# Fused attention and gated two-layer product on one core: held output sums, early units, split differences, and Tile's scheduler for all engines but TensorE

## The chip, the cores and the metric

The kernel runs on one core of a Trainium2 chip. The core has a TensorE (PE, with its weight loads listed apart as PEld), a VectorE (DVE), a ScalarE (ACT), a GpSimd (POOL), a SyncE (SP) that here only issues transfers, and 16 DMA engines. The metric is device time in microseconds (us). Before the change the median of three runs was 1395.18 us (1393.9 to 1398.31).

## The reference

The inputs are q, k and v of 8 batches x 8 heads x 576 positions x 64 numbers, and the weights w_in (512 x 2048) and w_out (2048 x 512), all float32.

```python
scores = scale * np.matmul(q, k.transpose(0, 1, 3, 2))      # scale = 1/8
mask = block_i >= block_j                                   # blocks of 64 positions
scores = np.where(mask, scores, -1000000000.0)
scores = scores - np.max(scores, axis=-1, keepdims=True)
attn = np.exp(scores)
attn = attn / (np.sum(attn, axis=-1, keepdims=True) + 1e-09)
x = np.matmul(attn, v)          # heads side by side: 4608 tokens x 512
h = x @ w_in
sp = np.maximum(h, 0.0) + np.log1p(np.exp(-np.abs(h)))
out = (h * erf(sp)) @ w_out
```

All products keep float32 accuracy. The kernel reaches it by splitting each number into a high part, which the cheap format holds exactly, and a low part, the difference; a product is then three products (high x high, high x low, low x high) added up in PSUM.

## The kernel before, in words

**Attention.** The 64 heads are 64 slots, n = 0 to 63. For head n, `load_qk` brings k and q into one of four buffers (st and qk): SP issues the loads and two copies (L450, L452, L453), POOL one load (L451), and POOL subtracts to get the low parts (kl at L456, ql at L457). `maxes` multiplies scores (s, L468), takes row maxima on DVE (L472, joined at L498), transposes them on PE (L502), and ACT copies them out of PSUM (mt, L504) and issues a transfer (L505) that puts them beside q as one more row of the contraction. The mask is also rows of that kind. `probs` then multiplies the transposed scores with the maxima already taken off (t, L521 and L522), ACT takes the exponential (p, L528) into one of two float32 buffers p32_0 (128 x 832) and p32_1 (128 x 768), and `split` makes the high half ph on ACT (L536) and the low half pl on DVE (L537), both in 16 bits. There is one copy of each p32 buffer. For a pair of heads `pv` multiplies by v (u, L567), and sums the rows (us, L593). Every four heads `normalise` transposes the sums and takes their reciprocal (rt L611, ri L614), spreads it (rw, ACT copies L621; transposes rb L629), multiplies (xs, DVE L632), splits the result (xs again: cast on ACT L634, difference on POOL L635) and sends it to DRAM (x_d, L636).

**The two-layer product.** w_in and w_out are cut into 16 weights of 128 hidden columns. `load_weight` splits each: SP loads it (raw, L285), DVE takes its bits apart (bits and sq, L287 to L297, ten operations of 128 x 512 for one weight), ACT squares and casts (L291, whi at L299) and POOL finishes the low part (wlo, L300 and L301). The work is done in two phases.

- Phase one holds 6 weights and runs over 18 tiles of 256 tokens. A tile has 3 units of 2 weights. A unit goes up (m_h, L342: 24 multiplications into one PSUM bank), through the gate, and down (o, L363: 12 multiplications into the tile's two output banks). The result of a tile is a partial sum; `store` copies it (ob, L670) to DRAM (part_d).
- Phase two holds the other 10 weights and runs over 9 tiles of 512 tokens, a unit being one weight. It adds the partial sums and writes the output.

The gate approximates h x erf(softplus(h)): ACT takes a tanh (L314) and four squares (L320), DVE joins (L324) and multiplies by h (L328), ACT casts to the high part gh (L329), POOL subtracts for the low part gl (L330).

**What sets the order.** Every instruction is a task with an engine, an estimated duration, its dependencies and a priority (`add`). `Plan.order` plays all tasks through a model of the engines: a free engine takes the ready task of lowest priority number, a result reaches another engine 200 ns after (`HOP`), and PE or a freed PSUM bank 500 ns later still (`SPARE`). The program is then written out in the model's order of start times, under a `manual_schedule`, so each engine issues in just that order. The eight PSUM banks and the numbered buffers are handed out in that model too. The last loop but one sets the priorities: slot n's steps lie between n and n + 1, the six weights of phase one are split in slots 1, 2, 3, 4, 7 and 8 (`W1`), and phase-one units are spread evenly over the slots by `spread`; those that are left when the heads end follow behind them. The five last of them (`TAIL`) use buffers that open only after attention.

## Time and profile before

| what | before |
|---|---|
| runs, median (lowest to highest) | 1395.18 us (1393.9 to 1398.31) |
| the profiled execution | 1394.03 us |
| its span, first to last instruction | 1392.3 us |
| mean granted TensorE clock | 0.922 |
| PE busy | 1254.5 us, 90% |
| PEld busy | 1038.4 us, 75% |
| DVE busy | 804.2 us, 58% |
| ACT busy | 973.5 us, 70% |
| POOL busy | 591.1 us, 42% |

The profile is of one execution; its times are counted from the first instruction. A group of instructions is named by its line in the kernel before, its engine, what it writes and what it reads, with buffer numbers left out. The granted clock says at what share of its full speed TensorE was let run in a stretch of time, and a duration of a multiplication is read together with it. A busy share of the whole span mixes stages in which different engines are the bound; the prediction therefore cuts the span into stages.

### The profile page before, as it was taken

The numbers are of one execution on the slowest core, as the hardware profiler recorded it, in microseconds if no ns is written. First come the engines' busy times: TensorE is split into PE (matmuls) and PEld (weight loads), VectorE is DVE, ScalarE is ACT, GpSimd is POOL, SyncE is SP. The second block draws the span as 40 slices with busy tenths as digits, with TensorE's granted clock in tenths as the row PEclk, the third lists the DMA queues.
The fourth block names the chain that finished last, engine by engine and source line by source line (L and its number), as shares of the span: only waits on it lengthen the run. The fifth ranks groups of instructions, "written<-read, shape, count | busy, mean of one in ns | idle before, by whom it ended". The sixth has DMA issues, their size and how long they took to land.

```text
span 1392.3 us, 22070 instructions
## 1 busy us (share of the span) xinstructions
PE 1254.5 (90%) x8168; PEld 1038.4 (75%) x8168; DVE 804.2 (58%) x1237; ACT 973.5 (70%) x1781; POOL 591.1 (42%) x456
## 2 busy tenths in 40 slices
PE   7456688889998999999999998779999999999997
PEld 3345576677777778788989987568888888888885
DVE  4988867888777788886532218953333233333232
ACT  1445557788776787789877768557677676776764
POOL 5666545576564566654432225632222222222221
PEclk9756778899999999999999999889999999999999
DMA  9556376787767677753473223203203113113010
GB/s 238 150 139 161 94 201 170 185 209 204 190 181 176 169 199 207 179 158 124 154 255 105 91 76 137 76 2 120 99 23 122 61 61 121 61 61 121 1 61 31
DMA packets 89372, 179.97 MB, mean 129 GB/s; under 512 B 8540, under 2 KB 27292, under 8 KB 89264
## 3 DMA queue, kind: packets, MB, share of 16 engines
q1 hardware_dynamic: 79280, 159.41, 38.5%
q0 software_dynamic: 9344, 18.97, 6.5%
q8 instruction: 65, 1.06, 0.3%
q10 hardware_dynamic: 640, 0.17, 0.1%
q14 instruction: 43, 0.35, 0.1%
HBM read 112.29 MB, written 37.75 MB: 108 GB/s over the span
## 4 chain that ended last, share of the span: by engine, by line
PE 53%; DVE 5%; ACT 2%; issue 1%; DMA 1%; DVEq 0%; ACTq 0%
PE o L363 25%; PE m_h L342 24%; DVE bits L287 1%; DVE bits L289 1%; PE u L567 1%; DVE m_r L324 1%; DMA qk<-mt 1%; PE t L521 1%; ACT m_r L320 1%; PE t L522 1%; PE s L468 1%; DVE sq L292 0%; DVE pl L537 0%; DVE bits L295 0%; PE rt L611 0%
## 5 line engine op out<-in xcount | busy, mean ns | idle before, releaser
L320 ACT ACTIVATE m_r<-m_r,c 128x512 f32<-128x512 f32 x576 | 406.3, 720 | 88.1 <-DVE m_r L324 61.6
L330 POOL TENSOR_TENSOR m_gl<-m_r,m_gh 128x512 fp32r<-128x512 f32 x144 | 189.0, 1314 | 511.8 <-ACT m_gh L329 298.4
L324 DVE SCALAR_TENSOR_TENSOR m_r<-m_r,m_r 128x512 f32<-128x512 f32 x144 | 125.6, 873 | 289.7 <-ACT m_r L320 268.7
L342 PE MATMUL m_h<-xh,whi 128*128 128x256 f32 (+1 forms) x648 | 208.9, 322 | 0.1
L342 PE MATMUL m_h<-xl,whi 128*128 128x256 f32 (+1 forms) x648 | 207.4, 320 | 0.0
L342 PE MATMUL m_h<-xh,wlo 128*128 128x256 f32 (+1 forms) x648 | 207.3, 320 | 0.0
L472 DVE TENSOR_REDUCE mx<-s 64x1 f32<-64x288 f32 (+4 forms) x384 | 163.9, 464 | 61.2 <-PE s L468 60.5
L528 ACT ACTIVATE p<-t 128x288 f32<-128x288 f32 (+4 forms) x384 | 135.3, 386 | 74.1 <-PE t L522 32.6
L363 PE MATMUL o<-whi,m_gh 128*128 128x512 f32 x432 | 173.7, 402 | 14.6 <-ACT m_gh L329 14.3
L521 PE MATMUL t<-qk 69*128 69x288 f32 (+4 forms) x384 | 136.3, 359 | 45.0 <-DMA qk<-mt 15.5
L328 DVE SCALAR_TENSOR_TENSOR m_r<-m_r,m_h 128x512 f32<-128x512 f32 x144 | 98.7, 685 | 134.5 <-ACT m_r L320 134.5
L363 PE MATMUL o<-wlo,m_gh 128*128 128x512 f32 x432 | 172.6, 400 | 0.0
L537 DVE TENSOR_TENSOR pl<-p,ph 128x832 f16<-128x832 f32 (+1 forms) x128 | 151.6, 1186 | 28.9 <-ACT ph L536 28.6
L468 PE MATMUL s<-qk 68*128 68x256 f32 (+3 forms) x384 | 119.4, 372 | 42.6 <-DVE mx L472 24.9
L314 ACT ACTIVATE m_r<-m_h,c 128x512 f32<-128x512 f32 x144 | 98.5, 684 | 78.1 <-PE m_h L342 77.2
L456 POOL TENSOR_TENSOR qk<-st,qk 64x576 fp32r<-64x576 f32 x64 | 106.6, 1669 | 69.8 <-DMA qk<-qk 40.0
L457 POOL TENSOR_TENSOR qk<-st,qk 64x576 fp32r<-64x576 f32 x64 | 108.1, 1688 | 60.9 <-DMA qk<-qk 57.7
L342 PEld LDWEIGHTS m_h<-xh,whi 128*128 128x128 f32 x648 | 124.5, 192 | 10.9 <-DVE mx L472 0.4
L342 PEld LDWEIGHTS m_h<-xl,whi 128*128 128x128 f32 x648 | 124.5, 192 | 10.0
L342 PEld LDWEIGHTS m_h<-xh,wlo 128*128 128x128 f32 x648 | 124.3, 192 | 8.5
L522 PE MATMUL t<-qk 128*128 128x288 f32 (+4 forms) x384 | 126.2, 333 | 0.0
L363 PE MATMUL o<-whi,m_gl 128*128 128x512 f32 x432 | 126.1, 394 | 0.0
(83 smaller groups left out, 2357.9 us busy)
## 6 DMA issues: line engine op xcount, KB each, us to landing
st<-qk SPq DMA_DIRECT2D x64, 288.0 KB
qk<-qk POOLq DMA_DIRECT2D x64, 288.0 KB, 4.8
qk<-qk SPq DMA_DIRECT2D x64, 288.0 KB
x_d<-xs SPq DMA_DIRECT2D x32, 576.0 KB
raw<-w SPq DMA_DIRECT2D x32, 512.0 KB
v<-v SPq DMA_DIRECT2D x16, 640.0 KB
qk<-qk SPq DMA_DIRECT2D x64, 144.0 KB
xh<-x_d SPq DMA_DIRECT2D x18, 512.0 KB
```

Source lines behind the costliest of these rows:

```text
L320: add("ACT", 722, lambda r=r, a=a, pp=pp: nc.scalar.activation(r[0](), a[0](), AF.Square, bias=const(pp[1]), scale=pp[0]), r=[a[1]], w=[r[1]])
L324: add("DVE", 890, lambda r=r, a=a, c=c, pp=pp, ops=ops: nc.vector.scalar_tensor_tensor(out=r[0](), in0=a[0](), scalar=pp[0], in1=c[0](), o ...
L330: add("POOL", 1450, lambda: nc.gpsimd.tensor_tensor(out=bgl(), in0=g[0](), in1=f32(bgh()), op=ALU.subtract), r=[g[1], bgh], w=[bgl])
L342: nc.tensor.matmul(hk()[:, k, :], lhsT=a(0)[:, cc * P : (cc + 1) * P], rhs=x()[:, cc, :], start=cc == 0 and i == 0, stop=cc == NCC - 1 and ...
L363: nc.tensor.matmul(o[c](), lhsT=a()[:, sl], rhs=b_(1), start=first and k == 0 and not lo and b_ is whi, stop=last and k == nu - 1 and lo)
L457: add("POOL", 1780, lambda: nc.gpsimd.tensor_tensor(out=t[D:, 1, :], in0=st()[D:, :], in1=f32(t[D:, 1, :]), op=ALU.subtract), r=[st], w=Q( ...
L468: add("PE", mmns(w_), lambda: nc.tensor.matmul(s()[:r, c0 : c0 + w_], lhsT=qh[:K, i * P : i * P + r], rhs=kh[:K, k0 : k0 + w_], start=True ...
L472: add("DVE", 145 + 1.07 * w_, lambda: nc.vector.tensor_reduce(out=mx[:r, col : col + 1], in_=s()[:r, c0 : c0 + w_], axis=AX.X, op=ALU.max, ...
L521: nc.tensor.matmul(s()[:kk, :w_], lhsT=kh[:K, ks], rhs=qh[:K, q0 : q0 + w_], start=True, stop=False)
L522: nc.tensor.matmul(s()[:kk, :w_], lhsT=klh[:, ks], rhs=qhl[:, q0 : q0 + w_], start=False, stop=True)
L528: add("ACT", 160 + 0.84 * (w_ - skip), lambda: nc.scalar.activation(p32s[pt][:kk, c : c + w_ - skip], s()[:kk, skip:w_], AF.Exp, scale=SCALE),
L537: add("DVE", 1250, lambda: nc.vector.tensor_tensor(out=pl(), in0=p, in1=ph(), op=ALU.subtract), r=keys + [ph], w=[pl])
```

## The change

The change has six parts.

- **Who orders.** `manual_schedule` now names PE alone. PE still issues in the order of the plan; for ACT, DVE, POOL and SP the scheduler of Tile, the layer in which the kernel is written, chooses the order.
- **Priorities in the plan.** `SPARE` is 300 in place of 500. ACT and DVE tasks that read PSUM go ahead by 0.7 (`DRAIN`), gates by 8 in place of 3 (`GATE`), PV products by 1.2 in place of 0.7.
- **Early units.** Phase-one units are no longer spread over the slots. They get priorities behind all attention work (`FILL` + their number), so the plan fills PE's gaps with them as early as their inputs are there; their gates get 10 + 1.1 for each unit. The weights of phase one are split in slots 2, 4, 6 and 8, and the last two when their first unit is planned.
- **Held sums.** For the first 14 tiles (`HT`) the down products of all three units are put off until the last unit's gate is planned, and are then written sorted by output bank.
- **Buffers.** Each p32 buffer exists twice (`NP`), gh and gl four times (`NG`, three before), r0 and r1 twice (`NR`, three before), xs once (`NX`, two before), ob once (two before). The gate no longer uses gl's buffer for an intermediate value.
- **Split differences.** pl of p32_0 stays on DVE, pl of p32_1 (128 x 768) goes to POOL. The rw copies and the xs cast go from ACT to DVE. The 16-bit unit matrix id16 is no longer made; its only use, the warming products at the start, read the other one's bytes.

```diff
-    SPARE = 500.0
+    SPARE = 300.0
+    DRAIN = -0.7
...
+        if eng in ("ACT", "DVE") and any((k[0] if isinstance(k, tuple) else k).tag[1] == "PSUM" for k in r if isinstance(k[0] if isinstance(k, tuple) else k, Buf)):
+            t.prio += self.DRAIN
...
-    GATE = -3.0
+    GATE = -8.0
+    NG, NR = 4, 2
+    HT = 14
+    NP = (2, 2)
+    NX = 1
...
-        bgh, bgl = (buf(gpool, [P, n], F32R, t, f"{name}_{t}") for t in ("gh", "gl"))
-        br = [buf("m", [P, n], F32, t, f"{name}_{t}") for t in ("r0", "r1")]
-        regs = [(br[0], br[0])]
-        free = [((lambda: f32(bgl())), bgl), (br[1], br[1])]
+        bgh, bgl = (buf(gpool, [P, n], F32R, t, f"{name}_{t}", NG if gpool == "m" else None) for t in ("gh", "gl"))
+        br = [buf("m", [P, n], F32, t, f"{name}_{t}", NR) for t in ("r0", "r1")]
+        regs, free = [(br[0], br[0])], [(br[1], br[1])]
...
-        plan.prio = at + GATE
+        plan.prio = at + GATE if when is None else when
...
-        for a in sorted(((k, c, lo) for k in range(nu) for c in range(tw // P) for lo in (False, True)),
-                        key=lambda a: (a[2], a[0], a[1]) if spread else (a[1], a[2], a[0])):
+        steps = [(a[1], lambda a=a: down(*a)) for a in sorted(((k, c, lo) for k in range(nu) for c in range(tw // P) for lo in (False, True)),
+                                                           key=lambda a: (a[2], a[0], a[1]) if spread else (a[1], a[2], a[0]))]
+        if held is not None:
+            held.extend(steps)
+            if not last:
+                return
+            steps = sorted(held, key=lambda s: s[0])
+            held.clear()
+        for c, f in steps:
             plan.prio += rate
-            down(*a)
+            f()
...
-    p32s = [spool.tile([P, n], F32, name=f"p32_{i}") for i, n in enumerate(PN)]
+    p32s = [[spool.tile([P, n], F32, name=f"p32_{i}_{j}") for j in range(NP[i])] for i, n in enumerate(PN)]
...
-            add("DVE", 1250, lambda: nc.vector.tensor_tensor(out=pl(), in0=p, in1=ph(), op=ALU.subtract), r=keys + [ph], w=[pl])
+            eng, ns, on = (("DVE", 1250, nc.vector), ("POOL", 2050, nc.gpsimd))[pt]
+            add(eng, ns, lambda: on.tensor_tensor(out=pl(), in0=p, in1=ph(), op=ALU.subtract), r=keys + [ph], w=[pl])
...
-    W1 = [1, 2, 3, 4, 7, 8]
+    W1 = [2, 4, 6, 8]
...
-    PV = -0.7
+    PV = -1.2
...
+            t, u = units1[0]
+            while len(w1) < 2 * u + 2:
+                plan.prio = n + 2 * u
+                next_w1()
+                plan.era = 0
+            unit1(FILL + NT // T * NU - len(units1), False)
...
-    with tc.manual_schedule():
+    with tc.manual_schedule(engines={mybir.EngineType.PE}):
```

How the change moves instructions is seen in the order in which each engine issues them. The rows give a line, an operation, what it writes, what it reads, and a shape; names carry the head, tile or unit and a running number. Lines of the changed kernel are up to some 15 higher.

On PE, behind head 40's last transposed scores (t2_40_256), before:

```order
L521 MATMUL t2_40_256_5596<-qk0_101 128x320
L522 MATMUL t2_40_256_5596<-qk0_101 128x320
L468 MATMUL s01_43_5600<-qk3_104 128x256 x2
L521 MATMUL t0_41_0_5604<-qk1_102 128x288
L522 MATMUL t0_41_0_5604<-qk1_102 128x288
L468 MATMUL s2_43_5608<-qk3_104 128x384
L521 MATMUL t0_41_288_5610<-qk1_102 128x288
```

and with the change:

```order
L535 MATMUL t2_40_256_5801<-qk0_101 128x320
L536 MATMUL t2_40_256_5801<-qk0_101 128x320
L349 MATMUL m1_4_2_h_5809<-xh256_1024_4238,whi4_2280 128x256
L349 MATMUL m1_4_2_h_5809<-xl256_1024_4240,whi4_2280 128x256
L349 MATMUL m1_4_2_h_5809<-xh256_1024_4238,wlo4_2318 128x256
L349 MATMUL m1_4_2_h_5809<-xh256_1024_4238,whi4_2280 128x256
```

Up products of tile 4's last unit (m1_4_2_h) now stand at this place. Counted over the whole list, 16 units up and 12 units down stood ahead of head 63's scores before, and 26.5 up and 24 down stand there now.

On DVE, the first rows (mx are row maxima, vm the largest value of v, bits and sq the weights' splitting), before:

```order
L401 CAST id16_124<-ident_74 128x128
L472 TENSOR_REDUCE mx0_120<-s01_0_179 128x1 x2
L472 TENSOR_REDUCE mx0_120<-s2_0_184 128x1
L412 TENSOR_REDUCE vm0_0_211<-v32_0_0_137 128x1
L472 TENSOR_REDUCE mx0_120<-s3_0_186 128x1
L472 TENSOR_REDUCE mx0_120<-s4_0_0_189 64x1
L472 TENSOR_REDUCE mx0_120<-s4_0_1_195 64x1
L498 TENSOR_TENSOR mx0_120<-mx0_120 64x1
```

and with the change:

```order
L426 TENSOR_REDUCE vm0_0_254<-v32_0_0_138 128x1
L294 TENSOR_SCALAR bits0_0_276<-raw0_0_141 128x512
L296 SCALAR_TENSOR_TENSOR bits0_0_276<-raw0_0_141,bits0_0_276 128x512
L294 TENSOR_SCALAR bits0_1_306<-raw0_1_143 128x512
L299 SCALAR_TENSOR_TENSOR sq0_0_194<-sq0_0_194,bits0_0_276 128x512
L296 SCALAR_TENSOR_TENSOR bits0_1_306<-raw0_1_143,bits0_1_306 128x512
L302 TENSOR_SCALAR bits0_0_276<-sq0_0_194 128x512
L299 SCALAR_TENSOR_TENSOR sq0_1_207<-sq0_1_207,bits0_1_306 128x512
L304 SCALAR_TENSOR_TENSOR bits0_0_276<-raw0_0_141,bits0_0_276 128x512
L302 TENSOR_SCALAR bits0_1_306<-sq0_1_207 128x512
L304 SCALAR_TENSOR_TENSOR bits0_1_306<-raw0_1_143,bits0_1_306 128x512
L486 TENSOR_REDUCE mx0_123<-s01_0_179 128x1 x2
```

The splitting of the first weight now stands ahead of head 0's maxima. Ahead of head 0's first pl stood one weight operation and now stand 29; ahead of the sixth head's stand 40 in both, since the last two weights of phase one have gone to heads 15 to 17.

On POOL, between heads 43 and 45 (qk are the low parts kl and ql, the DMA rows are loads that POOL issues, xs the second half of a split result), before:

```order
L456 TENSOR_TENSOR qk3_104<-st_43_5215,qk3_104 64x576
L457 TENSOR_TENSOR qk2_103<-st_42_5051,qk2_103 64x576
L457 TENSOR_TENSOR qk3_104<-st_43_5215,qk3_104 64x576
L451 DMA qk0_101<-qk 64x2x576
L451 DMA qk1_102<-qk 64x2x576
L456 TENSOR_TENSOR qk0_101<-st_44_5359,qk0_101 64x576
L456 TENSOR_TENSOR qk1_102<-st_45_5591,qk1_102 64x576
L457 TENSOR_TENSOR qk0_101<-st_44_5359,qk0_101 64x576
L635 TENSOR_TENSOR xs_4_1_0_5749<-xs_4_1_0_5749 128x576
```

and with the change:

```order
L470 TENSOR_TENSOR qk3_104<-st_43_5515,qk3_104 64x576
L471 TENSOR_TENSOR qk2_103<-st_42_5438,qk2_103 64x576
L552 TENSOR_TENSOR pl1_39_5807<-p32_1_1_114,ph1_39_5753 128x768
L465 DMA qk0_101<-qk 64x2x576
L471 TENSOR_TENSOR qk3_104<-st_43_5515,qk3_104 64x576
L470 TENSOR_TENSOR qk0_101<-st_44_5793,qk0_101 64x576
L552 TENSOR_TENSOR pl1_40_5959<-p32_1_0_113,ph1_40_5939 128x768
L337 TENSOR_TENSOR m1_4_1_gl_5991<-m1_4_1_r1_5805,m1_4_1_gh_5957 128x512
L471 TENSOR_TENSOR qk0_101<-st_44_5793,qk0_101 64x576
L465 DMA qk1_102<-qk 64x2x576
```

One pl of each head (pl1_39, pl1_40) now stands between these low parts and loads, and a gate's gl as well.

More of the change, by code (lines that the diff above doesn't have):

```diff
@@ L331, in gate, with moe_unit @@
         return bgh, bgl
-    def moe_unit(ws, xs, o, tw, nu, u, name, first, last, spread, oh, nh, gpool, at, rate, after=None):
+    def moe_unit(ws, xs, o, tw, nu, u, name, first, last, spread, oh, nh, gpool, at, rate, after=None, held=None, when=None):
         bh = bank(f"{name}_h")
@@ L399, in tile_attention_moe @@
         nc.gpsimd.memset(t, 0.0)
-    ident16 = spool.tile([P, P], F16, name="id16")
-    nc.vector.tensor_copy(ident16, ident)
+    ident16 = ident.bitcast(F16)[:, :P]
     def load_v(b, qd):
@@ L633, in m @@
                     r=[rb, (usbs[pp], 0), (usbs[pp], 1)], w=[(xs, hf)])
-            add("ACT", 670, lambda: nc.scalar.copy(xs()[:, 0, :], f32(xs()[:, 1, :])), r=[(xs, 0), (xs, 1)], w=[(xs, 2)])
+            add("DVE", 450, lambda: nc.vector.tensor_copy(xs()[:, 0, :], f32(xs()[:, 1, :])), r=[(xs, 0), (xs, 1)], w=[(xs, 2)])
             add("POOL", 1530, lambda: nc.gpsimd.tensor_tensor(out=xs()[:, 1, :], in0=f32(xs()[:, 1, :]), in1=f32(xs()[:, 0, :]), op=ALU.subtract), r=[(xs, 2)], w=[(xs, 0), (xs, 1)])
@@ L654, in tile_attention_moe @@
     units1 = [(t, u) for t in range(NT // T) for u in range(NU)]
-    os, hold = {}, {}
+    os, hold, held = {}, {}, []
     TAIL = 5
@@ L674, in unit1 @@
         t, u = units1.pop(0)
-        plan.prio = at
+        plan.prio = min(at, slot)
         for s in (t, t + 1):
-            if s in known and s not in x1:
+            if s in known and s not in x1 and (s == t or len(w1) == F1):
                 x1[s] = load_x("x", s * T, T)
@@ L682, in unit1 @@
         moe_unit(w1, x1[t], os[t], T, 2, u, f"m1_{t}_{u}", u == 0, u == NU - 1, not tail,
-                 hold[t], 3 if tail else NH, "g" if tail else "m", at, 0.05, marks.get(slot))
+                 hold[t], 3 if tail or t >= HT else NH, "g" if tail else "m", at, 0.05, None, held if t < HT else None, None if tail else LEAD + (t * NU + u) * GRADE)
         if u == NU - 1:
```

33 lines of the change are left out of this document (16 added, 17 removed).

## The prediction

> **What bounds the kernel now.** I read the page first, then PE's busy time by stages, then what PE waits for in each stage, then the cost of each group.
>
> ```profile
> span 1392.3 us, 22070 instructions
> PE   7456688889998999999999998779999999999997
> PEclk9756778899999999999999999889999999999999
> ```
>
> ```profile
> 0.00:200.00 200.00, 132.79 (x895) 99.18 (x896) 155.84 (x239) 91.93 (x195) 114.34 (x105) 0.71 0.65 164
> 200.00:640.00 440.00, 402.04 (x3734) 329.82 (x3733) 349.99 (x615) 342.67 (x752) 250.56 (x185) 0.92 0.70 181
> 640.00:850.00 210.00, 209.49 (x1343) 190.78 (x1343) 80.66 (x113) 165.55 (x264) 68.20 (x52) 1.00 0.39 134
> 850.00:930.00 80.00, 56.45 (x211) 44.13 (x210) 71.16 (x71) 46.65 (x76) 50.63 (x34) 0.85 0.23 78
> 930.00:1392.00 462.00, 453.72 (x1992) 374.49 (x1991) 146.53 (x202) 326.70 (x498) 107.41 (x83) 0.99 0.21 71
> ```
>
> The columns of the stages are PE, PEld, DVE, ACT, POOL, then the granted clock. There are five stages. Until 200 us the first heads and the weights go through DVE (155.84 of 200). From 200 to 640 us there is attention, with first-phase units between. From 640 to 850 us PE alone is the bound (209.49 of 210 at clock 1.00): the units that did not fit. From 850 to 930 us PE waits while DVE (71.16 of 80) prepares the last weights. After that PE is full again. So a unit taken out of the third stage saves its whole PE time, and the question is what it costs in the second, where PE has room: 38 us idle and a clock of 0.92.
>
> **Units moved out of the drain.** In the two listed orders of PE, the products ahead of head 63's scores are 16 units up and 12 units down before, and 26.5 up and 24 down now. The chain of waits has the price of each in the saturated stage:
>
> ```profile
> 761.80 2.87 PE m_h L342 x24
> 815.26 8.19 PE o L363 x36
> ```
>
> One unit up is 24 multiplications, 2.87 us; one unit down is 12, a third of 8.19, 2.73 us. So 10.5 x 2.87 + 12 x 2.73 = 30.1 + 32.8 = **62.9 us** leave the drain, on the path that sets the end.
>
> **What they cost in the attention stage.** PE does 402.04 x 0.92 = 370 us of full-speed work in 440 us there: 16% is room. With the moved units it has 433 us to do. How much room is left decides the sum. If 16% stays, the stage takes 433 / 0.84 = 515, that is +75, and the gain is gone with 12 us on top. The nearest row in which units are as dense is the end of that stage:
>
> ```profile
> 600.00:640.00 40.00, 38.01 (x408) 32.41 (x407) 30.37 (x47) 35.03 (x77) 18.19 (x12) 1.00 0.43 132
> 200.00:640.00 440.00, 50.65 (x168) 31.57 (x168) 0.92 0.70 181
> 200.00:640.00 440.00, 56.29 (x388) 51.82 (x387) 0.92 0.70 181
> 600.00:640.00 40.00, 5.12 (x12) 1.00 0.43 132
> ```
>
> The second and third row are the down products (L363) and the up products (L342) alone: 107 of 440 us, 24%. With 63 us more it would be about 36%. From 600 to 640 us the room is only 5% (38.01 of 40 at clock 1.00), but only 12 row maxima are left there (last row, L472 on DVE), so DVE and POOL are lighter than they will be. At 5% the stage takes 433 / 0.95 = 456, +16. I take 9%, nearer to this row because fillers that need nothing fresh also keep the clock up: 433 / 0.91 = 476, **+36 us**, ends +16 and +75.
>
> **Differences split between DVE and POOL, copies moved to DVE.**
>
> ```profile
> L320 ACT ACTIVATE m_r<-m_r,c 128x512 f32<-128x512 f32 x576 | 406.3, 720 | 88.1 <-DVE m_r L324 61.6 <-ACT mt L504 6.2 <-POOL m_gl L330 6.0
> L330 POOL TENSOR_TENSOR m_gl<-m_r,m_gh 128x512 fp32r<-128x512 f32 x144 | 189.0, 1314 | 511.8 <-ACT m_gh L329 298.4 <-PE o L363 162.2 <-DVE m_r L328 20.1
> L537 DVE TENSOR_TENSOR pl<-p,ph 128x768 f16<-128x768 f32 x64 | 69.5, 1085 | 7.0 <-ACT ph L536 6.8
> L621 ACT COPY rw<-ri 128x384 f32<-128x384 f32 x32 | 16.2, 507 | 9.0 <-PE rb L629 8.5 <-DVE ri L614 0.5
> L634 ACT CAST xs<-xs 128x576 fp32r<-128x576 f32 x32 | 21.3, 666 | 1.4 <-POOL xs L635 1.0 <-DVE xs L632 0.2
> L635 POOL TENSOR_TENSOR xs<-xs 128x576 fp32r<-128x576 f32 x32 | 46.9, 1472 | 26.3 <-ACT xs L634 19.3 <-issue 6.3 <-DMA qk<-qk 0.3
> ```
>
> ACT loses about 50 us (16.2 + 21.3 and the smaller rw copy) and gains 10.5 gates of about 4.2 us (four L320, the tanh and the gh cast), 44: even. DVE loses 69.5 us of pl and gains these copies, at most what ACT took for them: even or lighter. POOL gains 64 differences of 128x768. None is in the trace; POOL's own rows give 1314 ns at 512 and 1472 at 576 elements, 2.5 ns each, so 1.9 us at 768: 64 x 1.9 = 122 us. It lies beside other work (POOL is busy 250.56 of 440), but it stands between ACT's ph and the PV products, where DVE took 1.09 us. So every pair of heads has about 0.8 us less slack, and the PE order leaves between the last scores of head 41 and that pair's PV three sets of other products. POOL's queue also stops for data:
>
> ```profile
> POOL qk L457 <- DMA qk<-qk: 45.7, 19, 7.0
> POOL qk L451 <- PE t L522: 41.0, 16, 4.6
> POOL qk L456 <- DMA qk<-qk: 24.2, 12, 4.2
> ```
>
> (from 200 to 640 us). A pl that stands behind such a wait is late, and behind it the in-order PE. Nothing if Tile's order puts pl first, 32 pairs x 1 us at the other end; I take **+5 us**. The loads of later heads that POOL issues stand behind pl too:
>
> ```profile
> qk<-qk POOLq DMA_DIRECT2D x64, 288.0 KB, 4.8
> raw<-w SPq DMA_DIRECT2D x32, 512.0 KB
> ```
>
> Each lands in 4.8 us (first row) and is issued three heads ahead, 26 us at 8.8 us a head, which hides it; without that lead each late one costs up to those 4.8 us.
>
> DVE and POOL also hold each other up:
>
> ```profile
> 496.53 2.08 POOL L456 TENSOR_TENSOR qk<-st,qk 64x576 fp32r<-64x576 f32 x1
> 497.25 2.25 DVE L537 TENSOR_TENSOR pl<-p,ph 128x832 f16<-128x832 f32 x1
> L537 DVE TENSOR_TENSOR pl<-p,ph x128: 936/1008/2506, 35.3 to 629.2; 128x832 f16<-128x832 f32 x64, 128x768 f16<-128x768 f32 x64
> L330 POOL TENSOR_TENSOR m_gl<-m_r,m_gh x144: 1259/1294/1976, 248.8 to 1382.5; 128x512 fp32r<-128x512 f32 x144
> ```
>
> The DVE difference took 2.25 us instead of its median of about 1.0 and ended 0.9 us after POOL's. The two kinds run one after the other. The Trainium skill says so in "SBUF — State Buffer", section Who interferes with whom: DVE with two SBUF inputs and a GpSimd instruction that reads SBUF exclude each other for the whole instruction. The trace agrees (2.25 against 1.0). By that rule moving pl to POOL frees nothing, since both holders use the same port; that is the second rival below.
>
> **The start.** DVE's list now begins with the vm reduction and ten operations on the first weight, ahead of head 0's maxima; 29 weight operations stand ahead of head 0's difference, where one stood. But the last two of the six first-phase weights go to heads 15 to 17.
>
> ```profile
> 15.57 1.09 DVE L472 TENSOR_REDUCE mx<-s 128x1 f32<-128x128 f32 x3 [13.85 <-PE s L468]
> L289 DVE SCALAR_TENSOR_TENSOR bits<-raw,bits 128x512 int32<-128x512 int32 x32 | 37.4, 1169 | 0.9
> ```
>
> Ten such at up to 1.17 us would push head 0 back by 12 us, and on SP's queue the third weight's loads (two of the 512 KB above, 1 MB, 6.4 us at the first stage's 164 GB/s) now stand ahead of head 0's copies, within those 12; at the other end they fill the 13.85 us in which DVE waited, and twenty, some 20 us, leave a stage that DVE bounds. I take **-8**, ends -20 and +12.
>
> **Drain and transition.** In the drain before, 11 us or more of other PE work stand between a unit's up and its down product. Now some 7.5 us do (tile 12: unit 2 up, 12 down, 15 up, 12 down, 3 up). A gate alone takes 6.6 us from its tanh to gh:
>
> ```profile
> 1370.66 0.69 ACT L314 ACTIVATE m_r<-m_h,c 128x512 f32<-128x512 f32 x1 [0.82 <-PE m_h L342]
> 1376.69 0.61 ACT L329 CAST m_gh<-m_r 128x512 fp32r<-128x512 f32 x1
> ```
>
> Two gates share ACT there, so PE may wait up to 1 us for each of some 27 units: 0 to +27, I take **+8**. From 850 to 930 us PE waits for gates that stand behind weight work on DVE:
>
> ```profile
> PE o L363 <- ACT m_gh L329: 23.6, 6, 6.6
> ```
>
> Now the first four gates of phase two precede the last two weights on DVE, but the work is the same: 0 to -15, I take **-6**. The other buffer counts (xs and ob single, r0 and r1 double) cost at nothing: ACT is at 165.55 of 210 in the drain; without that slack a single ob costs 0.6 us for each of 18 tiles.
>
> **Sum.** -63 + 36 + 5 - 8 + 8 - 6 = -28 us against 1394.0 us, the profiled execution (span 1392.3 us): 1366. The median of the runs, 1395.2, is 1.2 higher; I say **1366 us**.
>
> **Rivals.** (1) PE's room is filled as in the last 40 us of attention and the start gains fully: -63 + 16 - 20 = -67, about 1327. For it: clock 1.00 wherever units are dense. Against it: DVE and POOL carry more than there.
> (2) Slower: the shared port and POOL's queue become the bound of attention.
>
> ```profile
> L456 POOL TENSOR_TENSOR qk<-st,qk x64: 1391/1423/2732, 14.6 to 604.2; 64x576 fp32r<-64x576 f32 x64
> L635 POOL TENSOR_TENSOR xs<-xs x32: 1397/1416/1900, 112.5 to 652.5; 128x576 fp32r<-128x576 f32 x32
> ```
>
> Per head, at undisturbed times (the middle of the three figures, in ns), the holders were POOL 2 x 1.4 (kl and ql), half an xs 0.7, 0.3 gates x 1.3, and DVE two pl 2.0 and about 0.7 of gates, maxima and weights: 6.6 of 8.8 us (50 heads in 440). Now POOL 3.5 + 1.9 + 0.5 x 1.3 and DVE 1.0 + 0.9 + about 0.2 for copies: 8.2. If the pair cannot be kept fuller than 83%, a head takes 9.9 us, the stage 494, +54; with starts and drain at their bad ends (+12, +20) and -63 that is +23, about 1417. It decides once a head takes over about 10 us. For it: POOL's stops above. Against it: until 640 us no wait of PE for a pl stands among those that the profile shows.
> (3) The change does not do what it says: Tile's order of ACT, DVE and POOL differs from the one that PE's order was planned with, PE's room stays 16%, +75: -63 + 75 - 8 - 6 = -2, about 1392. Against it: the order is moved by some four places on average.
>
> **Chances.** Forecast (1340 to 1386) 0.48; rival 1 0.15; rival 2 0.21; rival 3 0.16. A measurement of this kernel tells 0.3% (4 us) from no change. Rival 3 divides evenly between slightly faster, same and slightly slower: faster 0.68, same 0.06, slower 0.26. The range leaves a tenth out at each side: 1322 to 1412; the forecast's own is 1340 to 1386.
>
> **What would show it.** The last head's mt copy, at 619 us before, comes between 640 and 660; the saturated stretch after it is some 60 us shorter; granted clock in attention above 0.95. POOL busy near 85% there. A wait of PE's u for pl on POOL over 30 us in sum, or heads at 10 us, would show rival 2; PE waits for gh in the drain above 20 us would show that term too small. The forecast is wrong if attention grows by more than 60 us.

## The result, and the profile after

The changed kernel took **1410.6 us** (median; 1409.1 to 1414.1), the kernel before 1394.5 in the same comparison: a ratio of 1.0114, 95% interval 1.0085 to 1.0144. It is slower by 1.1%, where 1366 us and faster was forecast.

The page of the changed kernel, beside the rows of the kernel before that the prediction shows:

```profile
span 1410.3 us, 21986 instructions
PE   6377887988998899899988998859999999999997
PEclk8667786999999899999998999989999999999999
```

To see where the time went, both spans are cut at the same four events: head 14's mt copy, head 63's mt copy, the last PV product, and the last down product of phase one. The next rows are the view of busy time by stretches; the columns are length, then PE, PEld, DVE, ACT and POOL busy, the granted clock, the DMA share and GB/s. The kernel before:

```profile
0.00:191.10 191.10, 123.89 (x852) 90.61 (x853) 149.52 (x230) 87.76 (x186) 108.70 (x100) 0.72 0.65 165
191.10:619.20 428.10, 390.88 (x3552) 322.02 (x3552) 343.08 (x604) 328.66 (x722) 245.91 (x183) 0.91 0.71 184
619.20:634.50 15.30, 15.05 (x188) 11.92 (x187) 10.52 (x15) 13.77 (x31) 6.76 (x5) 1.00 0.31 114
634.50:871.90 237.40, 229.84 (x1447) 207.59 (x1446) 104.69 (x138) 186.47 (x298) 87.63 (x64) 0.99 0.40 136
871.90:1392.30 520.40, 494.82 (x2139) 406.26 (x2137) 196.37 (x253) 356.85 (x546) 142.12 (x106) 0.98 0.20 68
```

The changed kernel:

```profile
0.00:180.50 180.50, 121.48 (x855) 87.04 (x856) 126.27 (x212) 77.01 (x166) 120.14 (x107) 0.72 0.63 160
180.50:675.60 495.10, 439.61 (x3891) 365.48 (x3890) 376.48 (x664) 332.42 (x717) 351.26 (x249) 0.93 0.67 176
675.60:710.60 35.00, 33.49 (x327) 29.52 (x326) 21.21 (x26) 28.52 (x56) 17.55 (x11) 0.97 0.35 117
710.60:903.50 192.90, 173.79 (x990) 150.88 (x991) 94.47 (x136) 133.03 (x215) 70.87 (x50) 0.94 0.39 134
903.50:1410.30 506.80, 483.16 (x2115) 398.76 (x2113) 166.66 (x232) 357.23 (x535) 138.54 (x105) 0.98 0.19 67
```

PE's work at full speed is busy time times granted clock, and what a stretch is longer than that is PE time lost to waiting or to a lower clock. The work did move as the lists said: the fourth stretch has 173.79 x 0.94 = 163 us of it, before 229.84 x 0.99 = 228. But the room stayed: in attention 495.1 - 439.61 x 0.93 = 86 us are lost, 17%, and before it was 428.1 - 390.88 x 0.91 = 72, 17% too. And the fourth stretch, which lost 10 us, now loses 30.

| stretch | before: length, lost | changed: length, lost | all listed (first experiment): length, lost |
|---|---|---|---|
| to head 14's mt | 191.1, 102 | 180.5, 93 | 170.1, 79 |
| to head 63's mt | 428.1, 72 | 495.1, 86 | 476.5, 65 |
| to the last PV product | 15.3, 0 | 35.0, 3 | 32.2, 3 |
| to phase one's last down product | 237.4, 10 | 192.9, 30 | 180.0, 17 |
| to the end | 520.4, 36 | 506.8, 33 | 505.1, 24 |

(The clock has two places, so a long stretch's loss is uncertain by 2 to 3 us. The last stretch holds the same 2115 products in the last two columns, yet by this count 473 us of work in one and 481 in the other, so losses there that differ by less than some 8 us can't be told apart.) The third stretch, for which the prediction had no term, is 20 us longer, with 17 us more of PE's work in it.

### The profile page after: what moved, and what is told of

Same layout as the page of the kernel before. It is cut to its first block, busy times and chain, and to the rows that moved or that the text cites. A ratio compares the mean times of both kernels' runs of the same rounds, so it can differ in the third digit from the quotient of the medians.

```text
span 1410.3 us, 21986 instructions
## 1 busy us (share of the span) xinstructions
PE 1251.5 (89%) x8168; PEld 1031.7 (73%) x8168; DVE 785.1 (56%) x1268; ACT 928.2 (66%) x1685; POOL 698.4 (50%) x521
## 4 chain that ended last, share of the span: by engine, by line
PE 39%; ACT 4%; DVE 4%; issue 2%; POOL 2%; DMA 1%; DVEq 0%; SPq 0%; ACTq 0%; POOLq 0%
PE o L370 20%; PE m_h L349 18%; ACT m_r L327 3%; DVE m_r L331 1%; POOL m_gl L337 1%; DMA raw<-w 1%; DVE bits L296 1%; ACT m_r L320 1%; DVE bits L294 1%; DVE sq L299 1%; DVE bits L304 1%; ACT m_gh L336 0%; DMA qk<-qk 0%; DVE m_r L335 0%; DVE bits L302 0%
## 5 line engine op out<-in xcount | busy, mean ns | idle before, releaser
L337 POOL TENSOR_TENSOR m_gl<-m_r,m_gh 128x512 fp32r<-128x512 f32 x144 | 194.1, 1348 | 473.0 <-ACT m_gh L336 455.2
L331 DVE SCALAR_TENSOR_TENSOR m_r<-m_r,m_r 128x512 f32<-128x512 f32 x144 | 112.2, 779 | 330.9 <-ACT m_r L327 309.8
L370 PE MATMUL o<-whi,m_gh 128*128 128x512 f32 x432 | 179.0, 414 | 39.2 <-ACT m_gh L336 37.8
L486 DVE TENSOR_REDUCE mx<-s 64x1 f32<-64x288 f32 (+4 forms) x384 | 160.6, 465 | 39.6 <-PE s L482 38.9
L542 ACT ACTIVATE p<-t 128x288 f32<-128x288 f32 (+4 forms) x384 | 130.9, 387 | 57.4 <-PE t L536 55.4
L535 PE MATMUL t<-qk 69*128 69x288 f32 (+4 forms) x384 | 129.9, 348 | 17.8 <-DMA qk<-mt 10.8
L370 PE MATMUL o<-whi,m_gl 128*128 128x512 f32 x432 | 131.8, 408 | 13.8 <-POOL m_gl L337 13.7
L370 PEld LDWEIGHTS o<-whi,m_gh 128*128 128x128 f32 x432 | 84.8, 196 | 62.7 <-ACT m_gh L336 42.5
L470 POOL TENSOR_TENSOR qk<-st,qk 64x576 fp32r<-64x576 f32 x64 | 98.0, 1534 | 64.4 <-issue 23.5
L336 ACT CAST m_gh<-m_r 128x512 fp32r<-128x512 f32 x144 | 88.5, 615 | 53.9 <-DVE m_r L335 49.9
L552 POOL TENSOR_TENSOR pl<-p,ph 128x768 f16<-128x768 f32 x64 | 113.8, 1779 | 18.3 <-ACT ph L550 16.2
```

What stands on the lines that cost most here:

```text
L331: add("DVE", 890, lambda r=r, a=a, c=c, pp=pp, ops=ops: nc.vector.scalar_tensor_tensor(out=r[0](), in0=a[0](), scalar=pp[0], in1=c[0](), o ...
L337: add("POOL", 1450, lambda: nc.gpsimd.tensor_tensor(out=bgl(), in0=g[0](), in1=f32(bgh()), op=ALU.subtract), r=[g[1], bgh], w=[bgl])
L370: nc.tensor.matmul(o[c](), lhsT=a()[:, sl], rhs=b_(1), start=first and k == 0 and not lo and b_ is whi, stop=last and k == nu - 1 and lo)
L486: add("DVE", 145 + 1.07 * w_, lambda: nc.vector.tensor_reduce(out=mx[:r, col : col + 1], in_=s()[:r, c0 : c0 + w_], axis=AX.X, op=ALU.max, ...
L535: nc.tensor.matmul(s()[:kk, :w_], lhsT=kh[:K, ks], rhs=qh[:K, q0 : q0 + w_], start=True, stop=False)
L542: add("ACT", 160 + 0.84 * (w_ - skip), lambda: nc.scalar.activation(p32s[pt][n % NP[pt]][:kk, c : c + w_ - skip], s()[:kk, skip:w_], AF.Ex ...
```

## The experiments

Theory T held that the listed order of PE was planned with an order of the other engines that Tile's scheduler doesn't keep; theory P, the second rival of the prediction, that the differences on POOL hold up the heads; theory U, that the room in attention can't be filled. Each ratio below is against runs of the kernel before on the same chip, with its 95% interval, and runs taken at different times are compared by these ratios.

### Whose order: all engines listed again

```diff
-    with tc.manual_schedule(engines={mybir.EngineType.PE}):
+    with tc.manual_schedule():
```

> The changed kernel (1410.6 us) with every engine issuing in the plan's order again; all else of the change stays. Theory T (the order that Tile's scheduler gives ACT, DVE and POOL is not the one that PE's list was planned with, so PE's room stays 17% in attention and gates come late in the drain): faster by 25 us or more, 1360 to 1385, PE waits for gh and gl in the drain under 5 us where they were 9.6. Theory P (the differences on POOL: the shared port and POOL's queue): no change, 1405 to 1416. Theory U (the room in attention can't be filled by units that come earlier, whoever orders): within 10 us of 1410, with the drain's waits gone.

1369.1 us, ratio 0.982 (0.976 to 0.988). T holds for this kernel: everything else of the change is in, and it is 2% faster than the kernel before. U falls, though not wholly: 65 of 476.5 us, 14%, are still lost in attention. Its stretches:

```profile
0.00:170.10 170.10, 125.97 (x855) 87.94 (x856) 136.22 (x212) 76.56 (x165) 125.32 (x107) 0.72 0.65 173
170.10:646.60 476.50, 438.28 (x3911) 368.49 (x3908) 398.18 (x665) 341.04 (x720) 353.55 (x248) 0.94 0.69 180
646.60:678.80 32.20, 29.32 (x305) 26.07 (x304) 15.96 (x21) 28.45 (x54) 13.35 (x9) 1.00 0.31 104
678.80:858.80 180.00, 166.73 (x992) 145.40 (x991) 91.12 (x125) 130.36 (x211) 71.03 (x51) 0.98 0.41 141
858.80:1363.90 505.10, 486.17 (x2115) 399.47 (x2113) 193.05 (x248) 353.49 (x541) 144.86 (x108) 0.99 0.21 71
```

The same multiplications to within some twenty lie in each stretch of both kernels; the order of the other engines lengthened the first, second and fourth stretch by 10, 19 and 13 us. A detail went against the expectation: PE's waits for gh in the fourth stretch did not vanish, but those for gl did. The waits of PE there, in sum, times and longest, of the changed kernel and then with all engines listed:

```profile
PE o L370 <- ACT m_gh L336: 12.7, 7, 4.8
PE o L370 <- POOL m_gl L337: 5.1, 4, 2.3
```

```profile
PE o L370 <- ACT m_gh L336: 11.5, 8, 7.2
PE o L370 <- POOL m_gl L337: 0.3, 2, 0.2
```

The same edit the other way round, in the kernel before:

```diff
-    with tc.manual_schedule():
+    with tc.manual_schedule(engines={mybir.EngineType.PE}):
```

> The kernel before (1394.5 us) with PE alone in the listed order and Tile's scheduler for the other engines, nothing else. Theory T: slower by 15 to 35 us, 1410 to 1430, most of it between 200 and 640 us. Theories P and U: 1390 to 1400, since the plan and the work on each engine are those of before.

1390.6 us, ratio 0.997 (0.993 to 1.000): no difference. T had expected 1410 to 1430 here, so it does not hold in general: Tile's order is not bad in itself. In the kernel before it made the stretch up to head 14's mt 18 us shorter and the attention stretch 14 us longer. So the loss belongs to the changed kernel's plan together with Tile's order; what in the plan makes it sensitive was not tested.

### The difference on POOL

In the changed kernel, and then with all engines listed:

```diff
-            eng, ns, on = (("DVE", 1250, nc.vector), ("POOL", 2050, nc.gpsimd))[pt]
+            eng, ns, on = ("DVE", 1250, nc.vector)
```

> The changed kernel with both differences on DVE again. Theory T: within 6 us of 1410.6. Theory P: faster by 20 us or more, 1375 to 1390; POOL's busy time between 200 and 640 us falls from 317 to about 235 us. If DVE is the bound instead, slower: 1415 to 1430.

> All engines listed (1369), and both differences on DVE. With Tile's order this edit cost 20 us. If the move to POOL gains because DVE sets the pace of a head: 1382 to 1395. If it gained only through Tile's order: 1364 to 1374. By the prediction's term (+5 for the move, so -5 for its undoing): 1360 to 1368.

1430.1 us, ratio 1.024 (1.019 to 1.029), against 1.0114; and 1397.7 us, ratio 1.003 (1.000 to 1.007), against 0.982. The move of pl to POOL **gains** 20 us in the one and 28 in the other. (The plan is made anew for the edit, but PE's order moves little: 24 units up instead of 25 stand ahead of head 63's mt copy.) P falls. Why the move gains is not shown: 64 differences of about 1.0 us leave DVE, but its busy time over the span fell only from 848.0 to 834.5 us with all engines listed, and from 814.5 to 785.1 with Tile's order, while POOL's rose by 108 and 97 us. On POOL the difference took 1.65 us in the median, a little under the 1.9 estimated (minimum, median and longest in ns):

```profile
L552 POOL TENSOR_TENSOR pl<-p,ph x64: 1627/1652/2981, 67.9 to 698.6; 128x768 f16<-128x768 f32 x64
```

The move alone, in the kernel before:

```diff
-            add("DVE", 1250, lambda: nc.vector.tensor_tensor(out=pl(), in0=p, in1=ph(), op=ALU.subtract), r=keys + [ph], w=[pl])
+            eng, ns, on = (("DVE", 1250, nc.vector), ("POOL", 2050, nc.gpsimd))[pt]
+            add(eng, ns, lambda: on.tensor_tensor(out=pl(), in0=p, in1=ph(), op=ALU.subtract), r=keys + [ph], w=[pl])
```

> The kernel before with the difference of p32_1 on POOL, nothing else; every engine in the listed order. Theory P: slower by 10 to 25 us, 1405 to 1420. Theory T: 1388 to 1400. By the prediction's term for it, +5 less what DVE gains: 1394 to 1400.

1392.8 us, ratio 0.998 (0.994 to 1.001): nothing. There it has one copy of each p32 buffer; what the second copy does in the changed kernel is measured below.

### Which engine's order

The changed kernel with one or two more engines in the listed order:

```diff
-    with tc.manual_schedule(engines={mybir.EngineType.PE}):
+    with tc.manual_schedule(engines={mybir.EngineType.PE, mybir.EngineType.DVE}):
```

and likewise with Activation, with Pool and SP, with SP, and with Pool.

> The changed kernel with PE and DVE in the listed order, ACT, POOL and SP by Tile's scheduler. All engines listed took 1369, PE alone 1410.6: 41 us are to be placed. Theory D (Tile puts the first weights' splitting on DVE ahead of the first heads' maxima, and row maxima late in every head): 1375 to 1392. If it lies in ACT or POOL: 1402 to 1415.

> The changed kernel with PE and ACT in the listed order, DVE, POOL and SP by Tile's scheduler. Theory A (ACT's share: exponentials and gates out of the order that PE needs, four squares of one gate standing between another's): 1375 to 1392, and waits of PE for gh in the drain under 3 us. If it lies in DVE or POOL: 1402 to 1415.

> The changed kernel with PE, POOL and SP in the listed order, DVE and ACT by Tile's scheduler. Theory Q (POOL's queue and the order of loads: weights' loads and low parts ahead of the heads' loads and differences): 1375 to 1392. If it lies in DVE or ACT: 1402 to 1415. If no single engine carries it, all three of these runs lie between 1390 and 1410.

> The changed kernel with PE and SP in the listed order, the others by Tile's scheduler. With POOL and SP listed it took 1376.8 of 1410.6; this tells which of the two. Theory S (on SP's queue the copies of a head's loads, L466, stand ahead of the next heads' st loads and wait there for POOL's load, 148.6 us against 64.7): 1376 to 1388. If POOL's own order is it: 1400 to 1412.

> The changed kernel with PE and POOL in the listed order, the others by Tile's scheduler. Theory S: 1398 to 1412, and SP's wait at L466 stays above 110 us. If POOL's own order is it (the splitting of weights, differences and loads out of turn): 1376 to 1390. If POOL's order sets SP's: 1376 to 1390 with SP's wait at L466 down to about 65 us.

| in the listed order beside PE | median us | ratio (interval) | against the changed kernel's 1.0114 |
|---|---|---|---|
| DVE | 1393.5 | 1.000 (0.998 to 1.003) | -1.1% |
| ACT | 1398.5 | 1.004 (1.001 to 1.008) | -0.7% |
| POOL | 1398.0 | 1.002 (0.999 to 1.006) | -0.9% |
| SP | 1411.5 | 1.015 (1.010 to 1.020) | +0.3% |
| POOL and SP | 1376.8 | 0.988 (0.983 to 0.993) | -2.3% |
| all | 1369.1 | 0.982 (0.976 to 0.988) | -2.9% |

No single engine carries it; DVE's and ACT's runs lie between the two ranges that were named for each. I had formed theory S from the waits of SP's queue: the copies of a head's loads (L466) stood ahead of later loads and waited for POOL's own load. In the changed kernel, and with SP listed, from 180 to 680 us:

```profile
SPq L466 <- DMA qk<-qk: 148.6, 40, 7.4
```

```profile
SPq L466 <- DMA qk<-qk: 66.8, 23, 7.4
```

The wait fell by 82 us and the time did not, so S falls: this wait alone does not set the time. Others of SP's waits grew with that order (that of L391, the loads of x, from 7.0 to 37.4 us). POOL and SP together gave more than the two alone (2.3% against 0.9% and none); why, I could not settle.

### Where in the program

Tasks before a time of the plan are written out with all engines listed, the others with PE alone, in three kernels (up to head 14, from head 14 to 63, from head 63 on):

```diff
+    tasks = plan.order()
+    lo, hi = 0.0, marks[14].at
+    for a, b, whole in ((0.0, lo, False), (lo, hi, True), (hi, 1e12, False)):
+        with tc.manual_schedule() if whole else tc.manual_schedule(engines={mybir.EngineType.PE}):
+            for t in (t for t in tasks if a <= t.at < b):
...
```

> The changed kernel with all engines in the listed order until head 14 in the plan, and PE alone from there. Read from the stages' lost PE time (length less busy times clock: 93.0 us against 79.4 with all listed) the start carries 14 us: 1392 to 1402. Cause tested: Tile puts the first weights' splitting and loads ahead of the first heads. If the start's delay is made good later (units wait there anyway): 1405 to 1414.

> The changed kernel with all engines listed from head 14 to head 63 in the plan, PE alone before and behind. By the stages' lost PE time (86.3 against 64.5) the middle carries 22 us: 1383 to 1395. If the heads' pace isn't set by the order but by DVE's load: 1404 to 1414.

> The changed kernel with PE alone listed until head 63 in the plan and all engines from there. By the stages' lost PE time (drain 29.5 against 16.6, the 70 us behind it 20.8 against 13.2) the end carries 20 us: 1385 to 1397. If drain and transition only wait for the last weights' splitting, which has the same work in both orders: 1403 to 1412.

1402.7 us, ratio 1.008 (1.005 to 1.012); 1392.3 us, 1.000 (0.997 to 1.002); 1400.2 us, 1.004 (1.001 to 1.007). Against 1.0114 that is -0.3%, -1.2% and -0.8%, together 2.2% of the 2.9%, and the rest is within the intervals. The middle came in its range; start and end came between the two named for them, with some 4 and 10 us where 14 and 20 had been read from lost PE time. All three stretches carry a part, the heads in the middle the largest. Each also shows up where it was put: the start takes 170.9 us, the stretch of the middle heads 480.4, and with the end listed, the stretch to phase one's last down product has the 180.0 us of the kernel with all engines listed:

```profile
715.70:895.70 180.00, 166.82 (x990) 145.44 (x990) 91.21 (x125) 130.22 (x211) 70.98 (x51) 0.98 0.41 141
```

How such an order loses time can be read at the start. The timeline of the changed kernel (start, duration, engine, line, and in brackets the idle time before and what ended it), DVE, then POOL, then PE:

```profile
26.33 0.26 DVE L512 TENSOR_TENSOR mx<-mx 64x1 f32<-64x1 f32 x2
36.64 1.48 DVE L294 TENSOR_SCALAR bits<-raw 128x512 int32<-128x512 int32 x1 [10.05 <-POOL wlo L308]
...
58.19 0.27 DVE L431 TENSOR_REDUCE vs<-vt 1x1 f32<-1x128 f32 x1
...
58.98 0.14 DVE L433 RECIPROCAL vs<-vs 1x1 f32<-1x1 f32 x1
```

```profile
29.82 1.40 POOL L471 TENSOR_TENSOR qk<-st,qk 64x576 fp32r<-64x576 f32 x1 [6.79 <-DMA qk<-qk]
31.29 2.49 POOL L307 TENSOR_TENSOR sq<-sq,whi 128x512 f32<-128x512 f32 x2
33.87 1.40 POOL L471 TENSOR_TENSOR qk<-st,qk 64x576 fp32r<-64x576 f32 x1
35.34 2.49 POOL L308 TENSOR_TENSOR wlo<-sq,bits 128x512 fp32r<-128x512 f32 x2
```

```profile
59.18 0.58 PE L440 MATMUL vb<-vs,onesrow 1*128 1x2 f32 x2 [18.45 <-DVE vs L433]
```

DVE's next instruction at 26.6 us is the second weight's bits (L294). It needs a buffer that POOL still reads for the first weight's wlo, and POOL first waits for a load. DVE issues in its list's order, so it idles 10.05 us. Nineteen operations on weights start from 36.64 to 57.86 us, some of which wait for POOL's wlo again, and only behind them comes a reduction of 0.27 us (L431), for whose result PE, also in its list's order, waits 18.45 us. With all engines listed the same reduction comes ahead of the second weight, at 35.48 us, and its chain ends 23 us earlier (10 of these are left when head 14's mt is reached):

```profile
35.48 0.27 DVE L431 TENSOR_REDUCE vs<-vt 1x1 f32<-1x128 f32 x1
35.79 0.14 DVE L432 TENSOR_SCALAR vs<-vs 1x1 f32<-1x1 f32 x1
35.96 0.15 DVE L433 RECIPROCAL vs<-vs 1x1 f32<-1x1 f32 x1
```

In the drain it is the gate's last step, on POOL, and then on PE:

```profile
739.49 1.46 POOL L307 TENSOR_TENSOR sq<-sq,qk 128x512 f32<-128x512 f32 x1 [5.31 <-ACT qk L306]
741.03 1.28 POOL L308 TENSOR_TENSOR qk<-sq,bits 128x512 fp32r<-128x512 f32 x1
742.26 1.72 POOL L337 TENSOR_TENSOR m_gl<-m_r,m_gh 128x512 fp32r<-128x512 f32 x1
```

```profile
740.54 0.50 PE L370 MATMUL o<-whi,m_gh 128*128 128x512 f32 x1 [2.88 <-ACT m_gh L336]
740.88 0.40 PE L370 MATMUL o<-wlo,m_gh 128*128 128x512 f32 x1
...
744.03 1.22 PE L370 MATMUL o<-whi,m_gl 128*128 128x512 f32 x2 [2.28 <-POOL m_gl L337]
745.05 0.63 PE L370 MATMUL o<-whi,m_gh 128*128 128x512 f32 x1
```

The gh cast ended near 740.5 us (PE's product at 740.54 waited for it), but gl began only at 742.26, behind a weight's subtraction that had kept POOL waiting and its sum. PE stopped for 2.88 and 2.28 us, and then ran slower: the product that took 0.40 us takes 0.63 from 745.05 us on.

For the middle heads I have no such single chain. PE's largest waits there, in the changed kernel, are for the last step of the maxima (L512) and for the gates of the early units:

```profile
PE mt L516 <- DVE mx L512: 13.5, 7, 3.7
PE o L370 <- ACT m_gh L336: 7.9, 6, 4.0
PE o L370 <- POOL m_gl L337: 7.4, 5, 2.7
```

With all engines listed they sum to 2.8, 0.6 and 2.3 us; there, on the other hand, PE waits 12.2 us for row maxima ahead of PV products (u on mx, L486), where the changed kernel has 0.7. So the waits only show which chains got longer, and do not add up to the 19 us.

### The plan's own parts, with all engines listed

One part at a time is undone in the kernel of 1369.1 us (ratio 0.982). The plan is made anew for each edit, so PE's order changes too: ahead of head 63's mt copy stand 25 units up and 24 down with all parts in, 22 and 21 without held sums, 21 and 18 with one copy of each p32 buffer, 24 and 21 with the weights' old slots, 22 and 21 with the copies on ACT. Each run prices a part together with the plan that goes with it.

Sums not held:

```diff
-    HT = 14
+    HT = 0
```

> All engines listed (1369.1) and no tile's sums held: each unit's down products follow its own gate. If holding is what makes the early units dense: 1380 to 1395. If it only moves the gates' wait to the drain (10 us of clear-cut lookahead there): 1360 to 1368. The theory that the units' place, not the holding, matters: within 6 us of 1369.

1371.2 us, ratio 0.986 (0.982 to 0.990): no difference that the intervals could tell. Holding the sums brings nothing in sum; it moves the loss. Without it the stretch of the heads loses 484.1 - 437.81 x 0.91 = 86 us, where 65 are lost with held sums, and the stretch to phase one's last down product loses 1 us, where 17 are lost:

```profile
693.70:863.40 169.70, 169.02 (x1025) 150.66 (x1026) 89.55 (x118) 130.28 (x210) 69.59 (x50) 1.00 0.44 151
```

One copy of each p32 buffer:

```diff
-    NP = (2, 2)
+    NP = (1, 1)
```

> All engines listed (1369.1) with one copy of each p32 buffer, as before the change. The prediction counted the buffers at nothing: 1365 to 1374. If the second copy is what lets a difference on POOL (1.8 us) stand without holding up the next head's exponentials: 1380 to 1395.

1419.8 us, ratio 1.019 (1.016 to 1.022): **51 us** slower. What ACT's exponentials wait for between 180 and 640 us, with one copy:

```profile
ACT p L542 <- PE t L536: 30.3, 29, 4.7
ACT p L542 <- POOL pl L552: 18.9, 9, 4.7
ACT p L542 <- DVE pl L552: 9.2, 6, 3.8
```

The second and third row are not there with two copies (what ACT's p waits for is PE, 24.6 us). With one, the next head's exponentials must wait until DVE or POOL has read the buffer: 28 us in sum. The plan with one copy also puts fewer units early, and how the 51 us divide between the waits and the other plan was not measured. The prediction gave the second copies no term at all.

The weights' slots as before the change:

```diff
-    W1 = [2, 4, 6, 8]
+    W1 = [1, 2, 3, 4, 7, 8]
```

> All engines listed (1369.1) with the six weights of phase one split in slots 1, 2, 3, 4, 7 and 8 again. The prediction's term for the start was 8 us of gain (bounds 20 and -12); the start's length fell by 21 us with all listed. If the weights' slots bring it: 1377 to 1390. If the lists' other changes bring it: 1364 to 1374.

1409.3 us, ratio 1.012 (1.008 to 1.017): 40 us slower. Only some 11 us of it are at the start (180.9 us to head 14's mt, against 170.1). The rest is spread over the heads and the drain, which is 203 us long instead of 180, since fewer units come early.

The copies on ACT as before the change:

```diff
-                add("DVE", 430 - 100 * hf, lambda hf=hf, k=k: nc.vector.tensor_copy(
+                add("ACT", 510 - 110 * hf, lambda hf=hf, k=k: nc.scalar.copy(
...
-            add("DVE", 450, lambda: nc.vector.tensor_copy(
+            add("ACT", 670, lambda: nc.scalar.copy(
```

> All engines listed (1369.1) with the rw copies and the xs cast on ACT again, as before the change. If DVE sets the pace of a head in the attention stage (moving pl to it cost 28 us, 64 x 1.0 us of work): DVE sheds 32 x about 1.3 us, faster by up to 15 us, 1354 to 1366. If ACT or POOL is as near: 1366 to 1374. If ACT is the bound: 1378 to 1390.

1380.3 us, ratio 0.992 (0.989 to 0.995): 1% slower. That speaks against DVE alone setting the pace of a head, for then it would have been a gain. The time falls in the range named for ACT as the bound; ACT is busy 341 of 476.5 us in attention with the copies on DVE, so it is not full, and why the copies cost there is not shown.

Units at the spread priorities:

```diff
-            unit1(FILL + NT // T * NU - len(units1), False)
+            unit1(max(n + BEHIND, 9 + BEHIND + (NT // T * NU - len(units1)) * spread), False)
```

> All engines listed and the units at the spread priorities of the kernel before, behind which they can't start early; the other parts of the change stay. By the prediction's terms for early units (62.9 us leave the drain, attention grows by 36): slower by about 25 us, 1385 to 1400. If PE's loss in attention goes by heads and not by the time the stage takes, the units are free there and undoing costs more: over 1400. If early units bring nothing and the split differences bring all: 1364 to 1375.

1429.0 us, ratio 1.027 (1.022 to 1.031). This run did not do what I meant. Without the old loop's break the units were not late: they ranked beside the heads, and more of them came early. Ahead of head 63's mt stood 42 units up (1008 multiplications), where the listed kernel has 25 (600), and that copy came at 789 us instead of 647.

```profile
169.50:789.00 619.50, 569.89 (x4583) 482.84 (x4582) 416.50 (x705) 418.88 (x839) 374.88 (x266) 0.88 0.57 155
```

619.5 - 569.89 x 0.88 = 118 us are lost there, where 65 are lost with the 25 units that fill gaps. How much of it is the units' rank and how much their number is not told, and what early units are worth against late ones this run doesn't tell either.

## Why the prediction was wrong

**The step that failed** is the third rival's dismissal: "Tile's order of ACT, DVE and POOL differs from the one that PE's order was planned with", to which the prediction gave 0.16, with "the order is moved by some four places on average" against it. With all engines listed the change takes 1369 us, near the forecast of 1366; Tile's order, with this plan, is the 41 us between that and 1410.6. In the sum, the term that failed by it is attention's: 9% of room was taken, and 17% stayed (14% with all engines listed). A mean displacement says nothing of the few places where an instruction that waits for a buffer comes ahead of one for which PE waits: nineteen weight operations, held up by a buffer, kept PE idle for 18.45 us at one place. The rival's time, 1392, was too low as well. It let PE's room stay, which is what happened (17% before and after; +67 us of attention for the +75 reckoned), but had nothing for the drain's lookahead, where 20 us more were lost, and nothing for the third stretch, 20 us longer.

Term by term:

- **Units out of the drain, -62.9.** Right in the amount that moved: the fourth stretch lost 228 - 163 = 64 us of full-speed work. But 17 of these went no further than the third stretch, between head 63's mt copy and the last PV product, which grew from 15.3 to 35.0 us (32.2 with all engines listed). No term of the sum stands for it.
- **Attention, +36 (ends +16 and +75).** Measured +67 (428.1 to 495.1 us). With all engines listed +48.
- **POOL's difference, +5.** Wrong in sign: -20 us as changed, -28 with all engines listed. The Trainium skill's rule ("SBUF — State Buffer", section Who interferes with whom), by which such instructions of DVE and GpSimd exclude each other, holds for single instructions in the rows that the prediction showed; the prediction's inference, that moving the work between the two therefore frees nothing, does not hold here, though what it freed on DVE is small: 14 to 29 us of busy time.
- **The other buffers, nothing.** The sentence named xs, ob, r0 and r1, and passed over the second p32 copies, the largest of the parts undone one at a time: 51 us with all engines listed, its plan included.
- **The start, -8.** Measured -11 (191.1 to 180.5); with all engines listed -21. "Ten such at up to 1.17 us" was the wrong worry: what cost was not the operations but the buffer one of them waited for.
- **The drain's lookahead, +8 (0 to +27).** The loss there rose by 20 us, inside the bounds, and by 7 with all engines listed. That it comes from the held sums is borne out: without them, and with all engines listed, 1 us is lost. The sums of PE's waits there are below the 20 us named as a sign (12.7 for gh, 5.1 for gl), but the clock was lower as well: 0.94 granted, 0.99 before.
- **The transition, -6.** With the end of phase two, lost time fell from 36 to 33 us, which this count can't tell from none; the stretch became 14 us shorter, with 24 products fewer in it.

With the third stretch, the five lengths changed by -11, +67, +20, -45 and -14 us, +18 in sum for the forecast -28; with all engines listed by -21, +48, +17, -57 and -15, -28 in sum. So the forecast was near the listed kernel's time by parts that cancelled, not by parts that were right: no term for the buffers, a wrong sign for POOL's difference, and attention and start sized without them.

**The second rival** (slower, about 1417) came nearest in time and is refuted in mechanism. Heads did take the 10 us that it named as its point, 495.1 / 49 = 10.1. But POOL was busy 351.26 of 495.1 us, 71% and not 85%, PE's waits for pl on POOL were 6.4 us in all (over the whole span) and not over 30, and undoing the move made the kernel slower.

```profile
PE u L582 <- POOL pl L552: 6.4, 4, 3.5
```

## What to carry to other kernels

An order written for one engine can depend on the orders of the others: here the planned order for all engines took 41 us off, and in the kernel before the same switch made no difference, so measure both. Before costing a change of order, look in each queue for the first instruction that must wait for a buffer, and for what stands behind it, rather than at how far instructions moved on average. And work can gain by going to a slower engine: it did here with two copies of its buffer, and did not in the kernel before, which has one. Whether the second copy makes the difference is open: no run has the changed plan with one copy and the difference on DVE.

## What was not expected

A stop of PE can cost more than its length. After waits of 2.88 and 2.28 us, with four products between them, the 128x512 product took 0.63 us instead of 0.40, and the 128x256 ones 0.41 instead of 0.28 until 749.5 us:

```profile
749.11 0.41 PE L349 MATMUL m_h<-xl,whi 128*128 128x256 f32 x1
749.32 0.36 PE L349 MATMUL m_h<-xh,wlo 128*128 128x256 f32 x1
749.52 0.28 PE L349 MATMUL m_h<-xh,whi 128*128 128x256 f32 x1
749.64 0.28 PE L349 MATMUL m_h<-xl,whi 128*128 128x256 f32 x1
```

The starts are 0.21 us apart in the first two rows and 0.12 in the last two. The Trainium skill ("TensorE: Matmul & The Clock Gate", section Part 1: The HAM clock gate) tells of a state at half and one at full rate, the full one coming after about 3.4 us of sustained work. This trace agrees on the rates, with 0.21 against 0.12 us; here the slow rows last 5.5 us, from 744.03, where PE's work began again, to 749.5 us.

The best version found is the change with all engines in the listed order: 1369.1 us, 0.982 (0.976 to 0.988) of the kernel before. What stays open is why POOL and SP listed together give more than the sum of each, why the difference gains on POOL, and which chain loses the 16 us among the middle heads. The changed priorities (SPARE, DRAIN, GATE, PV) and the numbers of gh, gl, r0 and r1 were not undone one at a time.
